# Rounding float64 weights: the top words copied by GpSimd instead of ScalarE

## The chip, the cores and the metric

The kernel runs on one core of one Trainium2 chip. The metric is the device time of one execution in microseconds (us), from the first to the last instruction of the program; several executions are timed and the median is given. The engines that matter are TensorE (PE in the profile; its weight loads are PEld), VectorE (DVE), ScalarE (ACT), GpSimd (POOL) and the transfer queue of SyncE (SP). Each engine runs its own list of instructions in program order, and they wait for each other through semaphores.

## The reference

```python
# q, k, v: (8, 8, 576, 64)
scores = scale * np.matmul(q, k.transpose(0, 1, 3, 2))
kth = np.partition(scores, -32, axis=-1)[..., -32:-31]
scores = np.where(scores >= kth, scores, -1e9)
attn = softmax(scores)
x = (attn @ v) laid out as (4608, 512)
h = x @ w_in                      # (512, 2048)
out = np.maximum(0.01 * h, h) @ w_out   # (2048, 512)
```

It is top-32 attention over 64 heads, followed by a feed-forward layer with a leaky ReLU. The inputs q, k and v are float32. The two weight matrices reach the kernel as float64, seen by it as four 16-bit words per number, so the kernel first makes float32 numbers of them. That first part is what the change concerns.

## The kernel before, in words

**Weight rounding.** The two matrices are cut into 16 pieces of 128 x 1024 numbers (`NPIECE`), the first eight from `w_in`, the others from `w_out`. One piece of float64 is 1 MB; it is loaded into a tile `raw` of shape 128 x 1024 x 4 words, of which three buffers exist. `round_weights(n)` is a generator with three parts, separated by `yield`:

- Part one is on ScalarE. L118 copies the highest word of each number (sign, eleven exponent bits, four mantissa bits) into the tile `top`. L119 converts the second highest word into the destination, and L121 the lowest 32 bits into `m_low`.
- Part two is on VectorE and TensorE. L123 extracts the exponent from `top` into `scale`, L125 clamps it. Scaling turns the exponent into the bits of a bfloat16 power of two; for odd pieces ScalarE does it (L127), for even ones VectorE (L131). L128 takes the mantissa bits of `top` into `m_top`, L129 keeps only the sign in `top`. TensorE then adds the three mantissa parts in PSUM with multiples of the identity (L140, L141, L142), in two halves of 512 columns.
- Part three is on VectorE. L144 joins sign and scale, and L147 multiplies the sum in PSUM by it into the float32 weights.

The tiles `top` and `scale` have two buffers each, and `m_top` and `m_low` lie in a tile `wT` with three. The sums of pieces 0 to 12 use the two PSUM tiles `psc0` and `psc1`; the last three pieces use a pool of three PSUM buffers (`pw`).

The order is written out by hand. In step n of the first loop, part one of piece n, part two of piece n-1 and part three of piece n-2 are issued, and then the load of piece n+3:

```python
for i in (n, n - 1, n - 2) if AS_WORDS else ():
    if 0 <= i < NPIECE:
        if i == n:
            rounding[i] = round_weights(i)
        next(rounding[i], None)
load_weights(n + 3)
```

VectorE's list in the steady state is thus L123, L125, L128, L129 (and L131) of one piece, then L144 and L147 of the piece before it. Steps 6 to 9 also load four pairs of q and k. In step 15 the scores of the first two attention units are issued (L198 on TensorE, evicted by ScalarE at L207), ahead of the second part of the last piece.

**Attention and feed-forward.** The second loop runs over 144 units of up to 128 query rows of two heads. For each, VectorE takes the largest and smallest of pairs of scores (L216) and then finds the 32nd largest score in four rounds (L221, L224). GpSimd masks (L234, L235), ScalarE takes exponents, normalizes and splits words (L238, L250, L259), the transfer engines transpose, and TensorE weighs the values (L283). Between these, small steps of the feed-forward layer are put into the order of work by a budget (`mlp_steps`): L333 and L345 on TensorE. The first L216 stands in VectorE's list right after the last L147.

Of the kernel before, what the change touches and what calls it, by code (L numbers as in the profile page):

```python
# [13 lines left out]
ALU = mybir.AluOpType  # L14
# [5 lines left out]
def kernel(  # L20
# [13 lines left out]
    nc = tc.nc  # L34
# [45 lines left out]
    NPIECE = 2 * HP * DFF // WCH  # L80
# [3 lines left out]
    def piece(n):  # L84

        if n < NPIECE // 2:
            j, c = divmod(n, HP)
            return w_in[c][:, j * WCH:(j + 1) * WCH]
        f = 2 * (n - NPIECE // 2)
        return w_out[f // 4][:, f % 4:f % 4 + 2, :].rearrange("p g n -> p (g n)")  # L90
# [12 lines left out]
    def round_weights(n):  # L103

        raw = raw_of.pop(n)
        dst = piece(n)  # L110
        mid = raw[:, :, 2]
        low = raw.rearrange("p n w -> p (n w)").bitcast(U32).rearrange("p (n w) -> p n w", w=2)[:, :, 0]
        top = raws.tile([P, WCH], U16, name="top", bufs=2)
        scale = raws.tile([P, WCH], U16, name="scale", bufs=2)
        parts = work.tile([P, 2 * NKC - 1, P], F32, name="wT", bufs=3)
        parts = parts.rearrange("p c n -> p (c n)").bitcast(U16)
        m_top, m_low = parts[:, 0:WCH], parts[:, WCH:2 * WCH].bitcast(BF16)
        nc.scalar.copy(top, raw[:, :, 3])  # L118
        nc.scalar.activation(dst, mid, AF.Copy, bias=-7.0 - 2.0 ** -16, scale=2.0 ** -20)  # L119

        nc.scalar.activation(m_low, low, AF.Copy, bias=128.0, scale=2.0 ** -29)  # L121
        yield
        nc.vector.tensor_scalar(scale, top, 4, 0x7FF, ALU.logical_shift_right, ALU.bitwise_and)  # L123

        nc.vector.tensor_scalar(scale, scale, 1151.0, 896.0, ALU.min, ALU.max)  # L125
        if n % 2:
            nc.scalar.activation(scale, scale, AF.Copy, bias=-896.0 * 128, scale=128.0)  # L127
        nc.vector.tensor_scalar(m_top, top, 0xF, 0x3F80, ALU.bitwise_and, ALU.bitwise_or)  # L128
        nc.vector.tensor_scalar(top, top, 0x8000, None, ALU.bitwise_and)  # L129
        if n % 2 == 0:  # L130
            nc.vector.tensor_scalar(scale, scale, 896.0, 128.0, ALU.subtract, ALU.mult)  # L131
        if n < NPIECE - 3:
            pw = ps_sc.tile([P, 2, 512], F32, name=f"psc{n % 2}")
            sums = [(pw[:, h, :], h * 512) for h in range(2)]
            ends = [(pw.rearrange("p h n -> p (h n)"), 0)]
        else:
            ends = sums = [(ps_ml.tile([P, 512], F32, name="pw", tag="ml"), h * 512) for h in range(2)]
        for pw, c in sums:
            at = slice(c, c + 512)
            nc.tensor.matmul(pw, ident_top, m_top[:, at].bitcast(BF16), start=True, stop=False)  # L140
            nc.tensor.matmul(pw, ident, dst[:, at], start=False, stop=False)  # L141
            nc.tensor.matmul(pw, ident_low, m_low[:, at], start=False, stop=True)  # L142
        yield
        nc.vector.tensor_tensor(scale, scale, top, ALU.bitwise_or)  # L144
        for pw, c in ends:
            at = slice(c, c + pw.shape[-1])
            nc.vector.tensor_tensor(dst[:, at], pw, scale[:, at].bitcast(BF16), ALU.mult)  # L147
# [268 lines left out]
    with tc.manual_schedule():  # L416
# [12 lines left out]
        for n in range(NPIECE + 2):  # L429
# [6 lines that stand above are left out]
            if 6 <= n < 6 + HP:  # L436
                load_qk(n - 6)
            elif n == NPIECE - 1:
                for u in steps[0:2]:
                    scores(u)  # L440
            if n == NPIECE - 1:
                load_v(0)
                load_v(1)
# [108 lines left out]
```

## Time and profile before

| what | value |
|---|---|
| time, median of 3 runs | 1514.51 us (1513.94 to 1515.4) |
| span of the profiled run | 1512.7 us |
| TensorE busy | 1429.0 us, 94% |
| VectorE busy | 1330.4 us, 88% |
| ScalarE busy | 1121.5 us, 74% |
| GpSimd busy | 1079.5 us, 71% |
| L118, ScalarE, 16 copies | mean 1120 ns |
| L127, ScalarE, 8 scalings | mean 1051 ns |
| L131, VectorE, 8 scalings | mean 420 ns |

Busy times are sums over the whole span. [...] The rounding stage ends at about 79 us, where the first L216 starts.

### The profile page before, as it was taken

To read this page: it belongs to the slowest core of one execution; us is meant where nothing else is said; L and a number is where in the kernel's file an instruction comes from. 1 tells how busy PE (TensorE), PEld (TensorE's weight loads), DVE (VectorE), ACT (ScalarE), POOL (GpSimd) and SP (SyncE) were. 2 spreads that over 40 slices of the span, in tenths; PEclk is the share of its full clock that TensorE was granted. 3 is DMA by queue.
4 is the path that set the end of the run, shared out by engine and by line. 5 is a ranking of instruction groups with operands and counts; after the bars stand their busy time and mean duration, and the time that the engine had idled before them with its cause. 6 is when DMAs were issued, how large, how long until landed. Compare 5 with 4: busy or idle time off the path is not lost.

```text
span 1512.7 us, 24128 instructions
## 1 busy us (share of the span) xinstructions
PE 1429.0 (94%) x8030; PEld 934.5 (62%) x8032; DVE 1330.4 (88%) x3421; ACT 1121.5 (74%) x2149; POOL 1079.5 (71%) x726
## 2 busy tenths in 40 slices
PE   5736988999999999999999999999999999999998
PEld 2314545767676766676767676767666766666774
DVE  6899899999999999899999998999999989999600
ACT  7846887878787877787878787878787777787720
POOL 0058788887878777778787787878887878788700
PEclk9965999999999999999999999999999999999999
DMA  7714466655655556656664565645755555555510
GB/s 283 282 31 125 119 169 182 161 139 143 186 154 151 128 164 158 174 126 156 173 169 137 141 159 168 171 132 149 186 157 150 134 158 154 151 140 136 140 52 14
DMA packets 399293, 227.03 MB, mean 150 GB/s; under 512 B 343360, under 2 KB 343360, under 8 KB 397120
## 3 DMA queue, kind: packets, MB, share of 16 engines
q1 hardware_dynamic: 399168, 225.49, 54.2%
q8 instruction: 63, 1.03, 0.3%
q14 instruction: 62, 0.51, 0.1%
HBM read 46.14 MB, written 94.37 MB: 93 GB/s over the span
## 4 chain that ended last, share of the span: by engine, by line
PE 84%; DVE 10%; ACT 3%; DMA 2%; issue 1%; SPq 0%; DVEq 0%; ACTq 0%
PE pz L345 31%; PE ph L333 31%; PE psc L198 10%; PE po L283 10%; DVE tops L221 4%; DVE pairs L224 3%; DMA wT<-apart 1%; DVE pairs L216 1%; PE ph L308 1%; DVE scale L144 1%; ACT split L259 1%; ACT scale L127 0%; ACT wT L121 0%; DVE w_in L147 0%; ACT s_sb L238 0%
## 5 line engine op out<-in xcount | busy, mean ns | idle before, releaser
L234 POOL TENSOR_SCALAR pen<-s_sb,tops 128x576 f32<-128x576 f32 x288 | 638.4, 2217 | 234.8 <-DVE tops L221 205.9
L221 DVE MAX8 tops<-pairs 128x8 f32<-128x288 f32 (+1 forms) x1152 | 635.8, 591 | 0.0
L345 PE MATMUL pz<-w_out,gT 128*128 128x512 f32 x1152 | 506.7, 595 | 0.0
L333 PE MATMUL ph<-x,w_in 128*128 128x256 f32 x2176 | 482.4, 381 | 0.0
L224 DVE MATCH_REPLACE8 pairs<-tops,pairs 128x288 f32<-128x288 f32 (+1 forms) x864 | 460.0, 537 | 0.0
L333 PEld LDWEIGHTS ph<-x,w_in 128*128 128x128 f32 x2176 | 408.9, 190 | 77.1 <-issue 19.8
L235 POOL TENSOR_TENSOR s_sb<-s_sb,pen 128x576 f32<-128x576 f32 x288 | 406.9, 1413 | 24.0
L345 PEld LDWEIGHTS pz<-w_out,gT 128*128 128x128 f32 x1152 | 215.9, 190 | 264.4 <-issue 263.5
L259 ACT COPY split<-s_sb 128x1152 uint16<-128x1152 uint16 x288 | 315.7, 1144 | 0.0
L207 ACT COPY s_sb<-psc 128x576 f32<-128x576 f32 x288 | 169.4, 639 | 108.9 <-PE psc L198 108.9
L250 ACT ACTIVATE s_sb<-s_sb,rz 128x576 f32<-128x576 f32 x288 | 206.7, 767 | 33.0 <-DVE rz L247 33.0
L238 ACT ACTIVATE s_sb<-s_sb,nbias 128x576 f32<-128x576 f32 x288 | 221.4, 769 | 11.5 <-POOL s_sb L235 11.5
L198 PE MATMUL psc<-kt,qt 64*128 64x288 f32 (+1 forms) x1280 | 198.5, 438 | 29.3 <-ACT s_sb L207 29.1
L216 DVE TENSOR_TENSOR pairs<-s_sb 128x576 f32<-128x576 f32 x288 | 213.7, 780 | 10.2 <-ACT split L259 0.5
L283 PE MATMUL po<-wT,vt 128*64 128x128 f32 (+1 forms) x3200 | 182.7, 271 | 22.7 <-DMA wT<-apart 22.7
L283 PEld LDWEIGHTS po<-wT,vt 128*64 128x64 f32 x3200 | 163.2, 140 | 54.7 <-issue 26.9
L198 PEld LDWEIGHTS psc<-kt,qt 64*128 64x128 f32 (+1 forms) x1280 | 110.9, 180 | 102.2 <-ACT s_sb L207 38.8
L339 ACT ACTIVATE gT<-ph 128x256 f32<-128x256 f32 x272 | 99.0, 380 | 94.6 <-PE ph L333 94.3
L232 POOL TENSOR_SCALAR nbias<-tops 128x2 f32<-128x2 f32 x144 | 33.5, 233 | 92.5 <-DVE tops L221 79.7
L247 DVE RECIPROCAL rz<-ze 128x2 f32<-128x2 f32 x144 | 22.4, 155 | 72.0 <-ACT ze L243 71.4
L297 ACT COPY x<-po 128x128 f32<-128x128 f32 (+1 forms) x160 | 32.5, 264 | 60.0 <-PE po L283 59.7
L224 DVE MATCH_VALUE_LOAD pairs<-tops,pairs 128x8 f32 x864 | 62.2, 72 | 0.0
(44 smaller groups left out, 378.3 us busy)
## 6 DMA issues: line engine op xcount, KB each, us to landing
apart<-split SPq DMA_DIRECT2D x288, 288.0 KB, 2.1
raw<-in_weights_dram SPq DMA_DIRECT2D x16, 1024.0 KB, 5.3
vt<-in_vk_dram SPq DMA_DIRECT2D x32, 320.0 KB, 3.6
qt<-in_qT_dram SPq DMA_DIRECT2D x32, 288.0 KB, 3.6
kt<-in_kT_dram SPq DMA_DIRECT2D x32, 288.0 KB, 4.1
out_dram<-o_sb SPq DMA_DIRECT2D x36, 256.0 KB, 2.0
wT<-apart SPq DMA_TRANSPOSE x144, 4.6
```

The source lines that it names most:

```text
L198: nc.tensor.matmul(ps[i][r0:r0 + u.rows, half, 0:HS], qt[d, u.q0:u.q0 + u.rows], kt[d, half * HS:(half + 1) * HS], start=True, stop=True,)
L216: nc.vector.tensor_tensor(pairs[:, :, n, :], u.both[:, :, 0:HS], u.both[:, :, HS:S], op)
L221: nc.vector.max(out=u.tops[:, i, r, :], in_=rest[i])
L224: nc.vector.match_replace(out=rest[i], in_to_replace=u.tops[:, i, r, :], in_values=rest[i], imm_value=LOWEST)
L234: nc.gpsimd.tensor_scalar(pen, u.s[i], u.tops[:, i, ROUNDS - 1, 7:8], MASKED, ALU.is_lt, ALU.mult)
L235: nc.gpsimd.tensor_tensor(u.s[i], u.s[i], pen, ALU.add)
L238: nc.scalar.activation(u.s[i], u.s[i], AF.Exp, bias=u.nbias[:, i:i + 1], scale=SCALE, accum_out=u.z[:, i:i + 1])
L250: nc.scalar.activation(u.s[i], u.s[i], AF.Copy, bias=0.0, scale=u.rz[:, i:i + 1])
L259: nc.scalar.copy(split, pairs[:, :, h])
L283: nc.tensor.matmul(po[side * D:(side + 1) * D, o, :], vt[:, c, side, :], u.wT[:, c + side * NKC if c + 1 < NKC else c, r:r + n], start=(c ...
L333: nc.tensor.matmul(ph[:, 0:n], w_in[c][:, f * P:(f + 1) * P], x[c][:, 0:n], start=(c == 0), stop=(c == HP - 1),)
L345: nc.tensor.matmul(pz[0:m, 0:DMODEL], gT[f][:, r0:r0 + m], w_out[f // 4][:, f % 4, :], start=(f == 0), stop=(f == NFC - 1),)
```

## The change

The copy of the highest words (L118) moves from ScalarE to GpSimd, which has no other work during the rounding. With ScalarE free of it, the scaling of the exponents goes to ScalarE in all pieces but the last, where before it was shared by odd and even pieces. In the last piece VectorE does it, since ScalarE has the evictions of the first scores ahead of that place. The purpose is to take work off the two engines that are busy in this stage and give it to one that is idle. In the changed file the lines after the scaling move: the mantissa bits (L128 before) are L130, the sign (L129 before) is L131, and VectorE's scaling of the last piece is L129. The numbers of other lines stay.

```diff
-        nc.scalar.copy(top, raw[:, :, 3])
+        nc.gpsimd.tensor_copy(top, raw[:, :, 3])
...
-        if n % 2:
+        if n + 1 < NPIECE:
             nc.scalar.activation(scale, scale, AF.Copy, bias=-896.0 * 128, scale=128.0)
+        else:
+            nc.vector.tensor_scalar(scale, scale, 896.0, 128.0, ALU.subtract, ALU.mult)
         nc.vector.tensor_scalar(m_top, top, 0xF, 0x3F80, ALU.bitwise_and, ALU.bitwise_or)
         nc.vector.tensor_scalar(top, top, 0x8000, None, ALU.bitwise_and)
-        if n % 2 == 0:
-            nc.vector.tensor_scalar(scale, scale, 896.0, 128.0, ALU.subtract, ALU.mult)
```

## The prediction

> **What bounds the kernel now.** I read the busy table by stage first, because an average over the whole span hides that the change touches only the first 80 us. Columns: stretch in us, its length, busy time of PE, PEld, DVE, ACT and POOL with instruction counts, granted clock, DMA share, GB/s.
>
> ```profile
> 20.00:40.00 20.00, 13.66 (x39) 5.32 (x40) 17.12 (x30) 16.88 (x17) 0.00 (x0) 1.00 0.73 248
> ...
> 79.00:100.00 21.00, 3.55 (x16) 1.94 (x16) 20.86 (x54) 4.25 (x9) 11.75 (x9) 0.64 0.00 0
> ...
> 400.00:800.00 400.00, 398.87 (x2355) 270.00 (x2354) 373.88 (x979) 309.74 (x607) 317.26 (x213) 1.00 0.59 157
> ```
>
> There are three stages. While weights are rounded, VectorE and ScalarE are both near 85% and GpSimd does nothing. From 79 us VectorE alone carries the top-k search. Later TensorE is full (398.87 of 400 us). Each stage follows the one before it in program order on its engine, so time taken off the rounding moves everything behind it forward by as much.
>
> Next, the timeline of the rounding stage, VectorE and ScalarE rows (start, duration, engine, line, operation, idle before and its releaser).
>
> ```profile
> 18.69 0.43 DVE L123 TENSOR_SCALAR scale<-top 128x1024 uint16<-128x1024 uint16 x1
> 19.15 0.43 DVE L125 TENSOR_SCALAR scale<-scale 128x1024 uint16<-128x1024 uint16 x1
> ...
> 19.49 0.42 DVE L128 TENSOR_SCALAR wT<-top 128x1024 uint16<-128x1024 uint16 x1
> 19.95 0.43 DVE L129 TENSOR_SCALAR top<-top 128x1024 uint16<-128x1024 uint16 x1
> ...
> 20.29 0.68 DVE L144 TENSOR_TENSOR scale<-scale,top 128x1024 uint16<-128x1024 uint16 x1
> ...
> 21.08 1.23 DVE L147 TENSOR_TENSOR w_in<-psc,scale 128x1024 f32<-128x1024 f32 x1
> ...
> 22.41 0.43 DVE L123 TENSOR_SCALAR scale<-top 128x1024 uint16<-128x1024 uint16 x1
> ...
> 24.11 1.06 ACT L127 ACTIVATE scale<-scale 128x1024 uint16<-128x1024 uint16 x1
> ...
> 25.21 0.69 DVE L144 TENSOR_TENSOR scale<-scale,top 128x1024 uint16<-128x1024 uint16 x1 [0.78 <-ACT scale L127]
> 25.94 1.11 ACT L118 COPY top<-raw 128x1024 uint16<-128x1024 uint16 x1 [0.76 <-DVE scale L144]
> ```
>
> The first seven rows are one step in which VectorE never waits: 22.41 - 18.69 = 3.72 us. The next step, up to the L123 at 27.34, takes 4.93 us: it has one more VectorE operation (L131) and waits 0.78 us for L127, which stands behind three ScalarE copies. L118 in turn waits for L144, which frees its buffer. This ring of L144, L118, L119, L121, L127 and L144 repeats every two pieces: (70.59 - 18.69)/12 = 4.325 us a piece from piece 3 to 15.
>
> The end of the stage, same view:
>
> ```profile
> 69.94 0.38 PE L140 MATMUL pw<-wT,ident_top 128*128 128x512 bf16 x1 [1.04 <-DVE w_out L147]
> ...
> 75.69 1.07 ACT L127 ACTIVATE scale<-scale 128x1024 uint16<-128x1024 uint16 x1
> ...
> 76.80 0.69 DVE L144 TENSOR_TENSOR scale<-scale,top 128x1024 uint16<-128x1024 uint16 x1 [2.53 <-ACT scale L127]
> ...
> 78.80 1.41 DVE L216 TENSOR_TENSOR pairs<-s_sb 128x576 f32<-128x576 f32 x2
> ```
>
> The last L127 queues behind the score evictions (L207), and VectorE idles 2.53 us. TensorE's last work on weights ends at 77.74, so it stands only just behind that wait.
>
> Finally, the GpSimd groups with shapes apart (busy, mean ns, idle), for the price of the new copy:
>
> ```profile
> L234 POOL TENSOR_SCALAR pen<-s_sb,tops 128x576 f32<-128x576 f32 x288 | 638.4, 2217 | 234.8 <-DVE tops L221 205.9 <-ACT s_sb L238 11.8 <-ACT o_sb L352 1.0
> L235 POOL TENSOR_TENSOR s_sb<-s_sb,pen 128x576 f32<-128x576 f32 x288 | 406.9, 1413 | 24.0
> ...
> masks.py:199 POOL TENSOR_SCALAR_AFFINE_SELECT ident<-ident 128x128 f32<-128x128 f32 x1 | 0.3, 295 | 0.1
> masks.py:197 POOL MEMSET ident<- 128x128 f32 x1 | 0.2, 205 | 0.3 <-POOLq L539 0.3
> ```
>
> **What the Trainium skill says.** "GPSIMD Engine Reference", section 3.1, gives 2.6 cycles an element for two inputs and 1.03 for a body of one or two operations, at 1.2 GHz. L235 agrees with the first: 576 x 2.6/1.2 = 1248 ns, and 165 ns of overhead make its 1413. For one input there is only the 128-element select: (295 - 165) x 1.2/128 = 1.2 cycles. Its section 7 puts a slower read (2.9 against 1.9 cycles) beyond a step of 8 bytes; every fourth uint16 is exactly 8, so just inside. No row of before shows that. "SBUF — State Buffer", section "Who interferes with whom": a VectorE operation in a two-port mode, or with two SBUF inputs against a reading GpSimd, locks GpSimd out, and the reverse. L123 to L131 would be such (0.43 us for 1024 elements is more than two elements a cycle), and L144 has two SBUF inputs; L147, which reads PSUM, would not. No trace here shows the lock at work in this stage, since GpSimd is idle in it.
>
> **The change part by part.**
> 1. *L118 leaves ScalarE.* Sixteen copies of 1.12 us go. A ScalarE step is then L119, L121 and L127, about 1.04 + 1.04 + 1.0 = 3.1 us (start to start, from the timeline), below VectorE's 3.72.
> 2. *L131 leaves VectorE in seven of the eight even pieces* (0.34 us each), and L127 is added on ScalarE there (1.05 us). All steps then have exactly the seven-row list above: 3.72 us. L127 of piece n-1 can start once its L125 is done; ScalarE runs some 3 us ahead of the L144 that needs it, so the 7.2 us that L144 waited (seven times, 2.53 at the end) go.
> 3. *The new ring.* Two `top` buffers: the copy for piece n+1 may not start before L144 of n-1 has read the buffer, and L123 of n+1 waits for it. On VectorE L144's end is 20.97 and the next L123 comes at 22.41: a gap of 1.44 us filled by L147. Of it about 0.15 goes to waking GpSimd and 0.1 to waking VectorE, so a copy up to T = 1.2 us is hidden; anything longer adds (T - 1.2) to every step. Behind the waiting L123 stands all of VectorE's step, and then TensorE (L140 waits for the mantissa at L130). In this place the copy meets only L147, not an operation that would hold the lock.
>    T is the unknown, and what follows are estimates; 1.03, 1.9 and 2.9 cycles are those of "GPSIMD Engine Reference". Low end: 1024 x 1.03/1.2 + 165 = 1.04 us. By the select's rate: 1024 x 1.2/1.2 + 165 = 1.19 us. By 1.9 cycles: 1.79. By L235's two-input rate: 2.38. By L234's rate, (2217 - 165)/576 = 3.56 ns: 3.8 us. I take 1.15: one input and no arithmetic should not cost more than the select.
> 4. *The start.* The first copy starts at 5.6 instead of 5.5; L123 at about 6.8 instead of 6.62. But two identity casts no longer stand between L123 and L125, so L128's successor (L130 in the changed file) ends at 8.02 as before, and TensorE, slow until 13.3 in both, sets the first L147. Step 2 loses L131: L123 of piece 3 at 18.35 instead of 18.69.
> 5. *The run of pieces.* L123 of piece 15 at 18.35 + 12 x 3.72 = 62.99 instead of 70.59.
> 6. *The end.* Piece 15's scaling is on VectorE, so it no longer waits for the evictions. What ends last is TensorE: the second half of piece 14 needs a PSUM buffer that the first L147 of piece 13 frees, at about 62.4 (69.94 before). From there the chain of half a piece, scores, evictions, scores and piece 15 took 77.74 - 69.94 = 7.80 us; hence 70.2, and the last half L147 ends at 70.9. The first L216 starts there instead of at 78.80: **7.9 us earlier**.
> 7. *Transfers.* Pieces of 1 MB every 3.72 us are 282 GB/s; with the four q/k pairs at pieces 6 to 9 it is 1.64/3.72 = 440 against some 390 measured from 42 to 54 us. Four steps so fall about 2 us behind. A piece has some 9.5 us from issue to need, and landing took 4.7 to 9.1 before, so I cost it at nothing, with up to 2 us in the range.
>
> Sum: 1514.5 - 7.9 = **1506.6 us**.
>
> **The rivals.**
> - *The copy becomes the ring* (T between 1.25 and 2.1 us). For it: the 1.9 cycles, and the step of 8 bytes at the very edge. Against it: the select's 1.2. At T = 1.5 it gives 1506.6 + 12 x 0.3 = 1510.2; at 1.79, 1506.6 + 12 x 0.59 = 1513.7, which can't be told from before. It breaks even at 1.2 + 7.9/12 = 1.86.
> - *Slower: GpSimd handles a strided 16-bit copy like its two-input or pointer operations*, or the port lock stretches it. At T = 2.38: 1506.6 + 12 x 1.18 = 1520.8; at 2.6 (2.9 cycles), 1523.4; at 3.8, 1538. For it: every long GpSimd row in this trace is at 2.6 cycles or more. Against it: those rows do two inputs or two operations.
> - *Transfers bind instead*: 2 us given back, 1508.6. For it: the 9.1 us landing at 50 us. Against it: nothing on ScalarE waited for a piece after the first.
>
> **How the numbers follow.** Copy hidden, with or without the transfer loss: 0.57 (1505 to 1509). Partly exposed up to T = 1.6: 0.15 (to 1511.5). T from 1.6 to 2.1: 0.14 (1511.5 to 1517.5). Beyond: 0.14. So faster 0.72, same 0.14, slower 0.14. The range runs from 1503.5, some us below the forecast for a start of the later stages that I can't foresee (their TensorE clock is 0.55 to 0.64 from 79 to 151 us), to 1517, which leaves out the slow copies.
>
> **What would show it.** Right: the copy near 1.15 us on GpSimd; L123 to L123 at 3.72; no wait of L144 for L127; the first L216 near 71 us; TensorE's stage from 400 us unchanged. Wrong: L123 waiting for GpSimd in every step (T over 1.2), L119 waiting for `raw`, VectorE operations longer than 0.43 us beside a running copy, or a first L216 near 71 with an end that has not moved.

## The result

| | before | after |
|---|---|---|
| time, median | 1514.95 us (1513.94 to 1516.49, 4 runs) | 1507.32 us (1505.46 to 1508.41, 4 runs) |
| span of the profiled run | 1512.7 us | 1506.6 us |
| first L216 | 78.80 us | 70.80 us |
| step, L123 to L123, pieces 3 to 14 | 4.325 us on average | 3.72 us |

The ratio is 0.9947, with a 95% interval of 0.993 to 0.9965: the kernel became faster by 7.6 us, half a per cent.

The busy table by stage of the changed kernel, for stretches that answer to those of before (stretch, length, busy time of PE, PEld, VectorE, ScalarE and GpSimd, clock, DMA share, GB/s):

```profile
20.00:40.00 20.00, 15.16 (x45) 5.93 (x44) 18.50 (x32) 16.07 (x16) 6.45 (x6) 1.00 0.88 332
...
71.00:92.00 21.00, 4.73 (x20) 2.25 (x16) 20.79 (x54) 4.30 (x9) 11.73 (x9) 0.59 0.00 0
...
400.00:800.00 400.00, 399.36 (x2332) 271.42 (x2329) 375.13 (x975) 311.87 (x612) 317.40 (x213) 1.00 0.57 155
```

VectorE rose from 17.12 to 18.50 us of the 20, and what is left are gaps of 0.03 to 0.11 us between some of its operations. In the later stretches the busy times are nearly as they were.

One steady step of the changed kernel, from its timeline:

```profile
19.89 0.69 DVE L144 TENSOR_TENSOR scale<-scale,top 128x1024 uint16<-128x1024 uint16 x1
...
20.64 1.14 POOL L118 COPY top<-raw 128x1024 uint16<-128x1024 uint16 x1 [2.58 <-DVE scale L144]
20.68 1.22 DVE L147 TENSOR_TENSOR w_in<-psc,scale 128x1024 f32<-128x1024 f32 x1
...
22.01 0.43 DVE L123 TENSOR_SCALAR scale<-top 128x1024 uint16<-128x1024 uint16 x1
...
22.93 1.06 ACT L127 ACTIVATE scale<-scale 128x1024 uint16<-128x1024 uint16 x1 [0.47 <-DVE scale L125]
...
23.61 0.68 DVE L144 TENSOR_TENSOR scale<-scale,top 128x1024 uint16<-128x1024 uint16 x1
```

The copy starts 0.06 us after L144 ends (20.58), runs for 1.14 us beside L147, and is done at 21.78, while L123 starts at 22.01. As L123 follows GpSimd's end by 0.03 us where it does wait (first piece: 6.62 to 6.65), 0.20 us are to spare. L144 shows no wait any more: L127 now waits for VectorE (0.47 us), not the reverse.

The end of the stage, same view:

```profile
62.35 0.38 PE L140 MATMUL pw<-wT,ident_top 128*128 128x512 bf16 x1 [0.41 <-DVE w_out L147]
...
68.90 0.69 DVE L147 TENSOR_TENSOR w_out<-pw,scale 128x512 f32<-128x512 f32 x1 [1.17 <-PE pw L142]
...
69.78 0.38 PE L142 MATMUL pw<-wT,ident_low 128*128 128x512 bf16 x1
...
70.19 0.69 DVE L147 TENSOR_TENSOR w_out<-pw,scale 128x512 f32<-128x512 f32 x1 [0.60 <-PE pw L142]
70.80 1.42 DVE L216 TENSOR_TENSOR pairs<-s_sb 128x576 f32<-128x576 f32 x2
```

VectorE now waits for TensorE (1.17 and 0.60 us), whose chain began at 62.35 with the wait for L147 of piece 13.

### The profile page after: what moved, and what is told of

It is laid out like the page before. It is cut to its first block, busy times and chain, and to the rows that moved or that the text cites. A ratio compares the mean times of both kernels' runs of the same rounds, so it can differ in the third digit from the quotient of the medians.

```text
span 1506.6 us, 24132 instructions
## 1 busy us (share of the span) xinstructions
PE 1427.3 (95%) x8032; PEld 933.2 (62%) x8032; DVE 1328.1 (88%) x3414; ACT 1111.2 (74%) x2140; POOL 1096.3 (73%) x742
## 3 DMA queue, kind: packets, MB, share of 16 engines
q8 instruction: 63, 1.03, 0.3%
## 4 chain that ended last, share of the span: by engine, by line
PE 85%; DVE 11%; DMA 2%; ACT 1%; issue 1%; POOL 0%; DVEq 0%; ACTq 0%; SPq 0%
PE pz L345 31%; PE ph L333 31%; PE psc L198 10%; PE po L283 10%; DVE tops L221 4%; DVE pairs L224 3%; DMA wT<-apart 2%; PE ph L308 1%; DVE pairs L216 1%; DVE w_in L147 1%; DVE scale L144 1%; DVE w_out L147 1%; DMA apart<-split 0%; ACT split L259 0%; DVE scale L123 0%
## 5 line engine op out<-in xcount | busy, mean ns | idle before, releaser
L234 POOL TENSOR_SCALAR pen<-s_sb,tops 128x576 f32<-128x576 f32 x288 | 637.5, 2214 | 238.0 <-DVE tops L221 211.0
L333 PE MATMUL ph<-x,w_in 128*128 128x256 f32 x2176 | 482.9, 381 | 0.0
L333 PEld LDWEIGHTS ph<-x,w_in 128*128 128x128 f32 x2176 | 409.3, 190 | 77.6 <-issue 20.2
L235 POOL TENSOR_TENSOR s_sb<-s_sb,pen 128x576 f32<-128x576 f32 x288 | 406.4, 1411 | 24.1
L216 DVE TENSOR_TENSOR pairs<-s_sb 128x576 f32<-128x576 f32 x288 | 213.5, 780 | 9.9
L283 PE MATMUL po<-wT,vt 128*64 128x128 f32 (+1 forms) x3200 | 181.4, 270 | 25.2 <-DMA wT<-apart 25.2
L283 PEld LDWEIGHTS po<-wT,vt 128*64 128x64 f32 x3200 | 162.1, 140 | 57.0 <-DMA wT<-apart 29.1
L352 ACT COPY o_sb<-pz 128x512 f32<-128x512 f32 x36 | 21.1, 586 | 53.9 <-PE pz L345 53.9
```

The source lines that it names most:

```text
L216: nc.vector.tensor_tensor(pairs[:, :, n, :], u.both[:, :, 0:HS], u.both[:, :, HS:S], op)
L234: nc.gpsimd.tensor_scalar(pen, u.s[i], u.tops[:, i, ROUNDS - 1, 7:8], MASKED, ALU.is_lt, ALU.mult)
L235: nc.gpsimd.tensor_tensor(u.s[i], u.s[i], pen, ALU.add)
L283: nc.tensor.matmul(po[side * D:(side + 1) * D, o, :], vt[:, c, side, :], u.wT[:, c + side * NKC if c + 1 < NKC else c, r:r + n], start=(c ...
L333: nc.tensor.matmul(ph[:, 0:n], w_in[c][:, f * P:(f + 1) * P], x[c][:, 0:n], start=(c == 0), stop=(c == HP - 1),)
```

## The experiments

Each is timed beside the kernel before on one chip; that kernel's median lay between 1514.77 and 1515.23 us in every set. Ratios are to it, with 95% intervals.

**The first half alone.** In the kernel before, only L118 moves:

```diff
-        nc.scalar.copy(top, raw[:, :, 3])
+        nc.gpsimd.tensor_copy(top, raw[:, :, 3])
```

> Only the first half of the change: the top words are copied by GpSimd, the scaling stays shared by odd and even pieces, and piece 15's is on ScalarE. Main theory (VectorE's own list is the bound once L144 no longer waits): a step of an even piece keeps VectorE's scaling and takes 3.72 + 0.34 = 4.06 us, one of an odd piece 3.72, so 7.78 for two; the last scaling again queues behind the evictions; first L216 at about 73.5 us, 5.3 earlier than before, time about 1509.6. Rival (the gain is all from unloading ScalarE): first L216 near 71 and the time of the whole change, 1507.3. Rival (the gain is from the scaling alone): near 78.8, 1515.

Measured: 1508.68 us, ratio 0.9963 (0.9951 to 0.9976). The steps are 4.05 and 3.72 us in turn, and the first L216 is at 72.87. So the step follows VectorE's own list to 0.01 us, and both rivals are out. Over the twelve steps from piece 3 to 15, which took 51.90 us before and 44.71 after, it took 46.70: the copy's move brings 5.2 of the 7.2 us that these steps gained. The first L216 is 5.9 us earlier than before because the start was 0.7 us shorter too: L123 of piece 3 stands at 17.96 instead of 18.69. This start varies where the code up to it is the same: it is 18.29 in the changed kernel, and 17.70 and 17.77 in the two runs below that alter only its end. In all of them the first L147 waits for TensorE; why TensorE is ready sooner in some stays open. In time the two kernels can't be told apart (1508.68 and 1507.32, with intervals that overlap); the stage tells them apart.

**The second half alone.** In the changed kernel, the copy goes back to ScalarE.

```diff
-        nc.gpsimd.tensor_copy(top, raw[:, :, 3])
+        nc.scalar.copy(top, raw[:, :, 3])
```

> Only the second half of the change: the copy stays on ScalarE, which scales in all pieces but the last. Main theory: the ring L144, L118, L119, L121, L127, L144 now takes 4.92 us in every step (before: in every other one), so L144 of piece 13 comes at 20.3 + 11 x 4.92 = 74.4 instead of 68.4 and the first L216 near 84.5; time about 1520.7, slower than before by 5.8. Rival (VectorE's list is what bound before, and taking L131 off it is the gain): first L216 at 76 to 78, time 1512 to 1514.

Measured: 1523.71 us, ratio 1.0058 (1.0046 to 1.0071), first L216 at 88.76. Its waits in the first 80 us (who waited for whom: total, times, longest) show VectorE behind ScalarE in every step:

```profile
DVE scale L144 <- ACT scale L127: 15.4, 14, 1.3
ACT top L118 <- DVE scale L144: 10.6, 14, 0.8
```

The step is 4.90 us against 4.92 expected. The end came 4.3 us later than I had worked out. Some 2.3 us are in the start: L144 of piece 2 was at 22.63, not 20.3, as the ring takes hold from the first piece. Another 2.3 us are in the end, where TensorE had half its clock from 78 to 82 us while it was on the chain. From its L140 at 78.00, which waits for L147 of piece 13, to the first L216 it took 10.76 us; in the changed kernel this was 8.45 (62.35 to 70.80). The slightly shorter step takes 0.2 us back.

```profile
78.00:82.00 4.00, 4.00 (x10) 1.85 (x11) 3.24 (x7) 3.31 (x4) 0.00 (x0) 0.50 0.00 0
```

So giving ScalarE more scaling is a loss by itself; it shortens the step only once the copy is gone from there.

**A longer copy.** In the changed kernel, half the words are copied a second time:

```diff
         nc.gpsimd.tensor_copy(top, raw[:, :, 3])
+        nc.gpsimd.tensor_copy(top[:, 0:512], raw[:, 0:512, 3])
```

> The changed kernel with the first 512 words copied a second time on GpSimd, so that the copy takes about 1.14 + 0.6 = 1.75 us in all. Main theory (the copy lies in a ring between L144 and the L123 two pieces on, with 0.20 us to spare): L123 now waits for GpSimd in every step, the step grows from 3.72 to about 4.13, twelve of them give 4.9 us; first L216 near 75.7, time about 1512.2. Rival (GpSimd has 2.58 us of idle time in a step, so a longer copy is hidden): step 3.72, first L216 at 70.8, time 1507.3.

Measured: 1514.91 us, ratio 0.9999 (0.999 to 1.0007), first L216 at 77.34. A step of it (lines are one higher, since one was added):

```profile
42.05 0.68 DVE L145 TENSOR_TENSOR scale<-scale,top 128x1024 uint16<-128x1024 uint16 x1
42.80 1.13 POOL L118 COPY top<-raw 128x1024 uint16<-128x1024 uint16 x1 [2.38 <-DVE scale L145]
...
43.99 0.65 POOL L119 COPY top<-raw 128x512 uint16<-128x512 uint16 x1
44.67 0.43 DVE L124 TENSOR_SCALAR scale<-top 128x1024 uint16<-128x1024 uint16 x1 [0.60 <-POOL top L119]
```

L124 (L123 of the changed kernel) waits 0.60 us for GpSimd in every step, though GpSimd itself is idle for 2.38 us of it. The step is 4.22 us. The copy takes 1.13 + 0.65 us with a gap of 0.06 between, so T is 1.84, and the gain in time is gone. That this lies next to the break-even of 1.86 in the prediction is partly luck. The first L216 still comes 1.5 us earlier than before, which is no more than the interval of the time allows; and the step grew by only 0.50 us (3.72 to 4.22), so the room was T up to 1.34, and the stage would break even near 1.34 + 8.0/12 = 2.0, an estimate from these numbers.

**The longer copy with a third buffer.** For every third piece `top` lies in a tile that is idle in this stage:

```diff
-        top = raws.tile([P, WCH], U16, name="top", bufs=2)
+        if n % 3 < 2:
+            top = raws.tile([P, WCH], U16, name="top", bufs=2)
+        else:
+            top = work.tile([P, S], F32, name="pen", bufs=1).bitcast(U16)[:, 0:WCH]
...
+        nc.gpsimd.tensor_copy(top[:, 0:512], raw[:, 0:512, 3])
```

> The doubled copy again (1.13 + 0.65 us), with a third buffer for the top words, so that the copy for piece n+1 waits for L144 of piece n-2 instead of n-1 and is done a step earlier. Theory of the ring alone: nothing waits for GpSimd any more, the step is back at 3.72 us, first L216 at 70.8, time about 1507.3. Theory of the shared port (a running GpSimd copy and a two-port VectorE operation exclude each other): the copy starts 0.06 us after L144 of n-2, runs 1.85 us, and so reaches 0.4 us into the next L123; that L123 or the copy is held up, the step stays near 4.15 and the first L216 near 76, time about 1512 to 1514, as with two buffers.

Measured: 1512.09 us, ratio 0.9985 (0.9976 to 0.9994), first L216 at 75.93, step 4.04 us. From its timeline (L122 is the second copy, L127 and L129 are L123 and L125 of the changed kernel):

```profile
39.60 0.64 POOL L122 COPY top<-raw 128x512 uint16<-128x512 uint16 x1
39.78 0.73 DVE L127 TENSOR_SCALAR scale<-pen 128x1024 uint16<-128x1024 uint16 x1
40.55 0.43 DVE L129 TENSOR_SCALAR scale<-scale 128x1024 uint16<-128x1024 uint16 x1
```

L127 works on another buffer than the running copy, shows no wait, and yet takes 0.73 us instead of 0.43: the copy ends at 40.24 and L127 0.27 us later, at 40.51. The first half alone has a longer meeting, once, at its start:

```profile
8.15 1.35 POOL L118 COPY top<-raw 128x1024 uint16<-128x1024 uint16 x1 [1.35 <-DMA raw<-in_weights_dram]
...
8.44 1.35 DVE L131 TENSOR_SCALAR scale<-scale 128x1024 uint16<-128x1024 uint16 x1
```

L131 of piece 0 needs nothing of this copy for piece 1, and takes 1.35 us instead of 0.42. It ends at 9.79, 0.29 us after the copy's end at 9.50. In both cases the VectorE operation ends 0.27 to 0.29 us after the copy, however long the two had run side by side, as if it were shut out until then and not merely slowed. The port theory holds, and the ring alone does not explain this kernel. The price is seen as a longer VectorE operation and not as idle time, so a table of waits would miss it.

**The last scaling on ScalarE.** In the changed kernel, timed once:

```diff
-        if n + 1 < NPIECE:
+        if n < NPIECE:
```

> The changed kernel with ScalarE scaling the last piece too. Theory (TensorE's chain ends the stage, the wait for L127 stands just ahead of it): L127 of piece 15 starts after the second unit's evictions at about 68.1, L144 at 69.2, and both halves of L147 run from 69.9; first L216 at about 71.25, 0.45 us later than in the changed kernel. Rival (this exception is what took the 2.5 us wait away): first L216 near 73.

Measured: 1506.91 us in one run, first L216 at 70.62.

```profile
67.52 1.07 ACT L127 ACTIVATE scale<-scale 128x1024 uint16<-128x1024 uint16 x1
...
68.62 0.69 DVE L144 TENSOR_TENSOR scale<-scale,top 128x1024 uint16<-128x1024 uint16 x1 [2.53 <-ACT scale L127]
...
70.62 1.42 DVE L216 TENSOR_TENSOR pairs<-s_sb 128x576 f32<-128x576 f32 x2
```

This run had reached the L123 of piece 15 at 62.42, 0.58 us ahead of the changed kernel's 63.00, all of it in the start (17.70 and 18.29). From there to the first L216 it took 8.20 us against 7.80: 0.40 more, and as much as before (8.21). The 2.53 us wait is back and costs hardly anything, since TensorE ends just behind it. The exception for the last piece is right but worth 0.4 us of the stage.

**Scores one step earlier.** In the changed kernel:

```diff
-            elif n == NPIECE - 1:
-                for u in steps[0:2]:
-                    scores(u)
+            if NPIECE - 2 <= n < NPIECE:
+                scores(steps[n - NPIECE + 2])
```

> The changed kernel with the scores of the first attention unit issued one step earlier (step 14), so that one set of scores and evictions leaves TensorE's chain at the end of the rounding. Main theory (this chain, from the second half of piece 14 on, ends the stage): piece 15's second half then waits for the PSUM buffer that the first L147 of piece 14 frees at about 66.5, and the first L216 comes at about 69.0 instead of 70.8; time about 1505.6. Rival (VectorE ends the stage, or the evictions put into ScalarE's list delay L127 of piece 14): first L216 at 70.8 or later, time 1507.3 or more.

Measured: 1504.68 us, ratio 0.9931 (0.9917 to 0.9944), first L216 at 68.52; steps of 3.72 us as in the changed kernel. From its last L123 (62.47) it took 6.05 us instead of 7.80: 1.75 less, where 1.8 was expected. The other 0.5 us of the 2.3 lie in the start. TensorE's chain did end the stage of the changed kernel. Here it no longer does:

```profile
66.53 0.68 DVE L144 TENSOR_TENSOR scale<-scale,top 128x1024 uint16<-128x1024 uint16 x1
...
67.31 1.29 DVE L147 TENSOR_TENSOR w_out<-pw,scale 128x512 f32<-128x512 f32 x2
...
68.52 1.42 DVE L216 TENSOR_TENSOR pairs<-s_sb 128x576 f32<-128x576 f32 x2
```

The waits of 1.17 and 0.60 us ahead of L147 are gone, 1.77 together, which is the gain. VectorE now runs through to L216, so its own list ends the stage. The expectation still had TensorE end it, after a wait for the PSUM buffer. That wait is there (0.23 us, at 66.07), but TensorE is done at 67.52, before VectorE comes to that half: the number was right, the engine was not.

**One operation for the sign.** Built on the early scores:

```diff
-        nc.vector.tensor_scalar(top, top, 0x8000, None, ALU.bitwise_and)
...
-        nc.vector.tensor_tensor(scale, scale, top, ALU.bitwise_or)
+        nc.vector.scalar_tensor_tensor(scale, top, 0x8000, scale, ALU.bitwise_and, ALU.bitwise_or)
```

> The kernel with early scores, and the masking of the sign (L131) put into L144, as one VectorE operation with two steps. If that operation keeps L144's 0.69 us, the step falls by 0.34 to about 3.38 and the first L216 comes at about 64, time about 1500.5; transfers would then need 310 GB/s and may bind. If it runs [...] as L147 does (1.23 us, 0.54 more than L144), the step is 3.72 - 0.34 + 0.54 = 3.92, the first L216 near 71, time about 1507.

Measured: 1508.37 us, ratio 0.9953 (0.9941 to 0.9966), first L216 at 70.92, step 3.79 us (one of 4.22), between the two that were expected. The group of the new operation:

```profile
L143 DVE SCALAR_TENSOR_TENSOR scale<-top,scale 128x1024 uint16<-128x1024 uint16 x16 | 19.5, 1219 | 0.9 <-ACT scale L127 0.7
```

It takes 1219 ns, more than the two it replaces (427 and 685). Fewer operations were slower.

**No clamp.** Built on the early scores. L125 is left out, so exponents outside the clamp's bounds would no longer be limited on VectorE; the weights here have none.

```diff
-        nc.vector.tensor_scalar(scale, scale, 1151.0, 896.0, ALU.min, ALU.max)
```

> The kernel with early scores, without the clamp of the exponents (L125), which none of these weights needs. Main theory (VectorE's list sets the step until something else does): the list falls from 3.72 to about 3.3 us; ScalarE's three operations take 3.1 and the ring with the copy 1.23 + 1.3 + 0.7 = 3.2, so both just fit; first L216 near 63.5 if transfers keep up, time about 1500. Rival (transfers bind next: 1 MB in 3.3 us is 318 GB/s, and 1.64 MB with q and k, 497, against about 390 measured): ScalarE or GpSimd waits for pieces in the middle of the stage, some 2 to 4 us, first L216 at 65.5 to 67.5, time 1502 to 1504.

Measured: 1502.74 us, ratio 0.9925 (0.9911 to 0.9938), first L216 at 63.61. Most steps are 3.26 us, and two are longer: 3.68, with an idle time of 0.53 us for which the profile names only VectorE itself, and 3.96. From its timeline around the second (L143 and L126 are L144 and L127 of the changed kernel):

```profile
48.84 1.16 ACT L119 ACTIVATE w_out<-raw 128x1024 f32<-128x1024 uint16 x1 [1.61 <-DMA raw<-in_weights_dram]
...
50.93 1.04 ACT L126 ACTIVATE scale<-scale 128x1024 uint16<-128x1024 uint16 x1
...
52.00 0.69 DVE L143 TENSOR_TENSOR scale<-scale,top 128x1024 uint16<-128x1024 uint16 x1 [0.61 <-ACT scale L126]
```

A late piece holds L119 for 1.61 us, and through L126 that reaches VectorE as 0.61 us. Both theories have a part: VectorE's list still sets most steps and the end is where the main theory had it (63.5), and transfers begin to show. Of all kernels tried this one has the lowest median, but its interval overlaps that of the early scores.

## Why the prediction was right

1. *L118 off ScalarE, and steps of 3.72 us.* Right: the list has six operations (the seventh row is the first of the next step), and twelve steps from piece 3 to 15 took 63.00 - 18.29 = 44.71 us, predicted 44.64. The first half alone shows it again with its 4.05.
2. *The copy's time.* T was the unknown; I took 1.15 us from the 128-element select. Measured:

```profile
L118 POOL COPY top<-raw 128x1024 uint16<-128x1024 uint16 x16 | 18.2, 1137 | 43.2 <-DVE scale L144 37.6 <-DMA raw<-in_weights_dram 5.6
```

   Two lengths, 1137 ns for 1024 and 649 for 512, give 0.95 ns an element and 161 ns of overhead. With the 1.2 GHz of "GPSIMD Engine Reference" (the Trainium skill), section 3.1, this is an estimate of 1.14 cycles, near that section's 1.03 and below the 1.9 and 2.9 of the rivals. No copy with another step was run, so what the step of 8 bytes costs is not shown. The 165 ns of the prediction were what was left over of L235's 1413, so its agreement with 2.6 cycles was no test; the 161 measured here support it. The section's 1.03 does not hold for every body of two operations: L234 does two on one tensor (with scalars from `tops`), and the prediction's 3.56 ns an element are 4.3 cycles by the same clock.
3. *The new ring with room up to T = 1.2.* The ring is there; the room was mis-sized by a little. The wake-ups are 0.06 and 0.03 us, not 0.15 and 0.1, so T up to 1.34 is hidden. The lines of before had their like: L144 ends at 25.90 and L118 of ScalarE starts at 25.94. The longer copy shows what the rival "the copy becomes the ring" would have given: 1514.91 us.
4. *The port.* "SBUF — State Buffer" (the Trainium skill), section "Who interferes with whom", says that a two-port VectorE operation and a GpSimd operation exclude each other. The prediction held that the copy meets only L147, which doesn't take the port; so it was in the changed kernel from the third copy on, where L123 stays at 427 ns and L147 at 1225, as before. The third buffer, which moves the copy's tail into L123, shows the exclusion at 0.73 us, and the first half alone once at 1.35.
5. *The end.* TensorE's chain from 62.35 (predicted 62.4) to the first L216 at 70.80 (predicted 70.9), confirmed by the last scaling on ScalarE and by the early scores. It rested also on a full TensorE clock in this chain, which the prediction took over from before without a word. The clock was 1.00 until 74 us, so this held, but it need not have: in the kernel before it was 0.57 from 64 to 68 us, when TensorE was not on the chain, and in the second half alone it was 0.50 on the chain and cost 2.3 us.
6. *Transfers cost nothing.* Right, with less room than the numbers look: ScalarE waited 3.9 us for pieces of `w_out`, up to 1.2 at a time, and none of it reached L144.
7. *Everything behind moves by as much.* Right in the median (7.6 of 8.0 us) and loose in single profiles; the profiled run was the slowest of its four (1508.41 us). Start of L216 before minus after is 8.0 us at unit 0, 7.24 at unit 9, 7.57 at 18, 4.71 at 24, 5.81 at 60 and 6.10 at 143. The 2.9 us lost from unit 18 to 24 are two waits of VectorE, of 1.64 and 1.03 us, that the kernel before does not have:

```profile
259.93 0.17 DVE L247 RECIPROCAL rz<-ze 128x2 f32<-128x2 f32 x1 [1.64 <-ACT ze L243]
...
278.78 0.17 DVE L247 RECIPROCAL rz<-ze 128x2 f32<-128x2 f32 x1 [1.03 <-ACT ze L243]
```

   VectorE came to this place 7.5 us earlier than before, but the others did not. ScalarE's L243 was 4.4 us earlier (259.69 against 264.10), behind evictions that wait for TensorE's L333, 5.0 us earlier (251.21 against 256.17). Ahead of that stands TensorE's L283, which waits for a transposing transfer, 5.3 us earlier. The lines, after and then before:

```profile
246.66 2.40 PE L283 MATMUL po<-wT,vt 128*64 128x128 f32 x20 [4.74 <-DMA wT<-apart]
```

```profile
251.95 2.40 PE L283 MATMUL po<-wT,vt 128*64 128x128 f32 x20 [5.17 <-DMA wT<-apart]
```

   TensorE's clock is low here in both kernels (0.50 and 0.76 from 245 to 255 us after, 0.56 and 0.76 from 248 to 258 before), but 2.2 of the 3.1 us between VectorE's 7.5 and ScalarE's 4.4 were gone when L283 started, and that waits for the transfer. What held the transfer was not tried and stays open. The last scaling on ScalarE, the one sign operation and the kernel without the clamp have two such waits each (0.94 to 1.26 us), the early scores one (0.83), the first half alone none. At unit 0 and unit 143 the differences to before are 5.93 and 6.20 us (first half alone), -9.96 and -9.15 (second half), 1.46 and 1.65 (longer copy), 2.87 and 4.32 (third buffer), 8.18 and 7.59 (last scaling), 10.28 and 9.38 (early scores), 7.88 and 6.44 (one sign operation), 15.19 and 13.70 (no clamp). So a gain of one engine in one stage is kept only as far as the engines that it waits for later have moved as well.

## What to carry to other kernels

Work moved to an idle engine is free only if it fits into the gap between the operation that frees its buffer and the one that needs its result; that gap (here 1.44 us, of which 1.34 could be used), not the idle time of the engine, is what its duration is to be compared with. Look also at what runs beside it: here the copy fell beside the one VectorE operation that leaves it the port, and a copy that reached 0.46 us into the next one (the third buffer) made that one 0.30 us longer. After such a move, ask which engine ends the stage: here it was TensorE's last chain, and moving one set of scores a step earlier brought another 1.75 us of the stage, after which VectorE's own list ended it.

## What the runs showed of the hardware

- A VectorE operation that meets a running GpSimd copy is not shown as waiting but as longer: 0.73 instead of 0.43 us and 1.35 instead of 0.42, each ending 0.27 to 0.29 us after the copy. The other way round, the changed kernel's second copy started at 8.04 us while the L131 of 7.91 to 8.34 was running, and took 1272 ns, where the least was 1100.
- `scalar_tensor_tensor` on two 16-bit tensors took 1219 ns for 1024 elements, where `tensor_tensor` on the same took 685.
- TensorE's clock can fall within the rounding: to 0.57 from 64 to 68 us in the kernel before, off the chain, and to 0.50 from 78 to 82 us in the run of the second half alone, on the chain that ended the stage. In the changed kernel it was 1.00 from 58 to 74 us.
